# A bilinear layer's two factors as one product of halves: seven multiplications in place of eight

## The chip, the cores and the metric

The kernel runs on one core of a Trainium2 chip. The metric is the device time of one execution, in microseconds (us). Three runs of the kernel before took 1200.35, 1203.59 and 1203.63 us; their median is 1203.59 us. A profile was taken of one more execution. In it every engine is seen separately: PE is the matrix engine (PEld its weight loads), DVE the vector engine, ACT the scalar engine, POOL the GpSimd engine, SP the engine that issues most transfers. A fixed program stands in each engine's queue and is worked off in order; engines wait for each other by semaphores.

## The reference, cut to what matters

Three layers follow each other on 4352 rows of 512 numbers (34 tiles of 128 rows):

```python
x = attention(x, state)                       # 8 x 8 heads, 512 + 32 positions each
x = moe(x)                                    # every row goes to one of 8 experts:
                                              #   relu(row @ w1[e]) @ w2[e], times a gate
a, b = x @ w1, x @ w2                         # both 512 -> 1024: the two factors
out = ((a * b) @ w3) @ w_out                  # 1024 -> 1024 -> 512
```

The kernel multiplies w3 and w_out into one matrix "wo" (1024 x 512) while the attention runs, so that the last layer is `(a * b) @ wo`. The rows' gates are squared and put on at the very end, and rows lie in the experts' order until the output is scattered back.

All matrix products are in 32 bits. Each operand is held as a pair, high part and rest (`split`, lines 169 to 172: ACT casts the high part, DVE subtracts to get the rest), and a product takes three matmuls: high by high, high by rest, rest by high (`passes`, lines 174 to 180).

## The kernel before, in words

Three stages run one after the other.

- The attention and the routing, to about 200 us. The change doesn't touch them.
- The experts, from about 200 to 625 us. Ten units of rows go through them: eight "quads" of 4 tiles (512 rows, or 576 in four of them, where 64 rows of another tile ride along) and two single tiles. `quad_first` makes 8 hidden chunks (one PSUM bank of the four called A each, or two with 288 columns each), ACT and DVE take them out; `quad_second` makes 4 output chunks in the two banks called C, which ACT copies out and writes to `y_T` in DRAM. After each chunk `fill` (line 1096) puts a piece of other work into the program. These pieces (`convert_wab`, `write_wab`, lines 913 to 924) fetch the bilinear weights, which come as 64-bit words, 512 columns at a time, turn them into 32 bits and write them to `wab_rows` in DRAM.
- The bilinear layer, from 630 us to the end. Between the two stages stands a branch (line 1192, `tc.If`), which is taken only if the rows need more than 38 tiles in all.

The bilinear stage holds all weights in on-chip memory, as pairs. It takes the rows in a first block of 2 tiles (256 columns) and eight of 4 tiles (512 columns). For each block and each of the 8 groups of 128 factor columns (f) it makes two products, pB (factor a) and pC (factor b), each of 4 chunks of 128 x 3 matmuls, ACT copies pB, DVE multiplies by pC, the product is split, and one step later 4 x 3 matmuls add `(a * b) @ wo` to four banks "po". At the block's end the four po are scaled by the gates and scattered to the output rows by indirect transfers from POOL (lines 1340 to 1349). Beside this, in its first blocks, DVE works out where each row goes (`places`, lines 1311 to 1323): 34 small matmuls "pput" and a run of DVE instructions.

What stands in which order in an engine's queue is set by a scheduler that plays the program with estimated times, under the constraints in the code (`issue_after`, data and buffers). SP, ACT and POOL issue transfers, each in its own order. A buffer with `bufs=1` is written again only when all readers of its last content are done, transfers included.

Of the kernel before, what the change touches and what calls it, by code (L numbers as in the profile page):

```python
# [52 lines left out]
def tile_attention_moe_bilinear(  # L53
# [54 lines left out]
    )  # L108
    TQ = PLUS
# [44 lines left out]
    wab_rows = dram.tile([2, DM, FF], F32, name="wab_rows")  # L154
# [19 lines left out]
    def passes(o, l, r, start, stop, here=False):  # L174

        for i, (a, b) in enumerate(((0, 0), (0, 1), (1, 0))):
            m = nc.tensor.matmul(o, l[a], r[b], start=start and i == 0, stop=stop and i == 2)  # L177
            if here:
                tc.keep_in_program_order(m)
        return m  # L180
# [6 lines left out]
    def load_f32(pool, name, src, tag, bufs, temps=None, tmp=2):  # L187

        n = src.shape[1]
        w = pool.tile([P, n], F32, tag=tag, name=name, bufs=bufs)  # L190
        if src.dtype != I64:
            nc.sync.dma_start(out=w, in_=src)
            return w
        raw = wr_raw.tile([P, n], I64, tag="raw", name=name + "_raw", bufs=RAW)
        eng("q_raw", 0, "sync").dma_start(out=raw, in_=src)
# [95 lines left out]
    c3 = ctx.enter_context(ExitStack())  # L291
    with ExitStack() as c1:
# [386 lines left out]
        c2.close()  # L679
        rings.append(Lines(c3.enter_context(tc.tile_pool(name="wr0", bufs=RING0, reuse_waits="tile"))))  # L680
        xp = Lines(c3.enter_context(tc.tile_pool(name="xp", bufs=3, reuse_waits="tile")))
# [191 lines left out]
    with ExitStack() as c2:  # L873
# [22 lines left out]
        def gate():  # L896
# [4 lines left out]
            gt = e3.tile([P, 2, NTT], F32, name="gt", bufs=1)  # L901
# [3 lines left out]
            zr = e3.tile([P, NTT], F32, name="zr", bufs=1)  # L905
# [7 lines left out]
        def convert_wab(i):  # L913

            i, j = divmod(i, 2)
            w, k = divmod(i, KD)
            at = slice(k * P, (k + 1) * P), slice(j * 512, (j + 1) * 512)
            t = load_f32(e3, f"wab{i}_{j}", (wa, wb)[w][at], "wab", 1, None, 1)
            unwritten.append((wab_rows[w][at], t))

        def write_wab():
            for o, t in unwritten:
                nc.scalar.dma_start(out=o, in_=t)
            unwritten.clear()

# [4 lines left out]
        def rows(tiles, n, gidx=gidx, s0=0):  # L930
# [4 lines left out]
                xp.tile([P, KD, QN if quad else P], F32R, tag=f"x{quad}{j}", name=f"x{j}_{s}", bufs=1 if quad else 2)  # L935
# [151 lines left out]
        converted = iter(range(4 * KD))  # L1087
        fills = itertools.cycle(kn("fills", "cw--"))

        def next_of(items, n, todo):  # L1090
            for i in itertools.islice(items, n):
                todo(i)

# [6 lines left out]
        def fill_():  # L1100
            if next(calls) < kn("from", 8):
                return
            c = next(fills)
            if c == "c":
                next_of(converted, 1, convert_wab)
            if c == "w":
                write_wab()

        def rows_T(pool, first, n, bufs):

            hl = [
                pool.tile([P, KD, QN if pool is xp else 512], F32R, tag=f"xTrue{j}", name=f"y{j}_{first}", bufs=bufs)
                for j in range(2)
            ]
            for k in range(KD):
                y = xp.tile([P, n], F32, tag="xg", name=f"yt{first}_{k}", bufs=4)
                nc.sync.dma_start(out=y, in_=y_T[:, k, first : first + n])
                split(*both(hl, slice(None), k, slice(0, n)), y)
            return hl
# [40 lines left out]
        for c, n in steps:  # L1160
            if c == "f":
                first_of(n)
            else:
                if n + 1 == len(units):
# [3 lines left out]
                    ahead = rows_T(xp, 0, P * (QT // 2), 1)  # L1168
# [3 lines left out]
        next_of(converted, 4 * KD, lambda i: (convert_wab(i), write_wab()))  # L1172
        c4.close()

        wab = [
            [
                chunk(f"wab{i}_{k}", wab_rows[i, k * P : (k + 1) * P].rearrange("p (h f) -> p h f", h=2))
                for k in range(KD)
            ]
            for i in range(2)  # L1180
        ]
        wo = [
            chunk(f"wo{k}", wo_rows[2 * k * P : 2 * (k + 1) * P].rearrange("(h p) f -> p h f", p=P))
            for k in range(KF // 2)
        ]


        if not kn("used", 1):
            used = nc.values_load(total, min_val=0, max_val=MAXT)
        e2 = Lines(c2.enter_context(tc.tile_pool(name="e2_more", bufs=2, reuse_waits="tile")))  # L1190
        e4 = Lines(c2.enter_context(tc.tile_pool(name="e4", bufs=2, reuse_waits="tile")))
        with tc.If(used > T0):  # L1192
# [6 lines left out]
            def run(tiles):  # L1199
                for s in tiles:  # L1200
                    u = QUADS + s - TB
                    e = expert(u)
                    w = load1(u, e, e4, 2), load2(u, e, e4, 2)
# [9 lines left out]


    with ExitStack() as c2:
        b2 = Lines(c2.enter_context(tc.tile_pool(name="b2", bufs=2, reuse_waits="tile")))
        blocks = [range(max(t, 0), t + NC_) for t in range(QT // 2 - NC_, NTT, NC_)]
        acc = {}
        ridx = b2.tile([P, NTT], I32, name="ridx", bufs=1)
        gd = b2.tile([P, NTT], F32, name="gd", bufs=1)  # L1220

        PIECE, LOOK = 6, 9

        spare = oh.rearrange("p t e -> p (t e)")
        place = spare[:, 0:NTT]
        block, within = [
# [82 lines left out]
        def places():  # L1311
# [7 lines left out]
            for a in pieces:  # L1319
                put(a, o)  # L1320
                if a % (2 * PIECE):
                    yield
            yield taken(o)

        def nothing():
            while True:
                yield
# [84 lines left out]
```

## Time and profile before

| what | value |
| --- | --- |
| median of three runs | 1203.59 us (1200.35 to 1203.63) |
| the profiled execution | 1204.63 us, span in the trace 1202.8 us |
| mean granted TensorE clock | 0.989 of 2.4 GHz |
| PE busy | 1154.7 us, 96% |
| DVE, ACT, POOL busy | 515.6, 426.3, 183.4 us (43, 35, 15%) |
| expert stage ends, bilinear stage starts | 625.03 us, 630.27 us |
| last matmul ends | 1192.20 us |
| DRAM read and written | 97.03 MB, 33.55 MB |

How to read it: PE is busy nearly all the time, so a row's worth lies in what it makes PE do or wait for. A matmul's duration in the trace overlaps with its neighbours', so the price of one is taken from the distance between the starts of groups, not from its own length. An ACT or DVE row with a number in square brackets had its engine idle that long, and the arrow names what ended the wait.

### The profile page before, as it was taken

Reading aid. Unit: us, or ns where it says so; the run is one execution under the profiler, and the core shown is the slowest. Engines: PE = TensorE matmul, PEld = TensorE weight load, DVE = VectorE, ACT = ScalarE, POOL = GpSimd, SP = SyncE. Lnnn points to the kernel's source line nnn. Section 1 sums busy time; section 2 is a strip of 40 time slices with the busy share of each in tenths; the row PEclk is TensorE's granted clock in tenths of the full one; section 3 lists DMA queues with packets and bytes.
Section 4 is the critical chain, followed back from the end, with each engine's and each line's share of the span. In section 5 each row is a group of like instructions: output and inputs, shape, how many; then the busy total and the mean of one; then the engine's idle time right before and its main releaser. Section 6 shows DMA issues by size and latency. Waiting matters only on the chain.

```text
span 1202.8 us, 17604 instructions
## 1 busy us (share of the span) xinstructions
PE 1154.7 (96%) x6928; PEld 984.1 (82%) x6928; DVE 515.6 (43%) x999; ACT 426.3 (35%) x764; POOL 183.4 (15%) x183
## 2 busy tenths in 40 slices
PE   6898999999999999999989999999999999999996
PEld 4665777989999999888869888888888888888885
DVE  4999796543545454544347513112221312121211
ACT  3787544433545444544332212121121212121111
POOL 2655235102121112010000001010000101010101
PEclk9899999999999999999999999999999999999998
DMA  7776427545475546574332101001020202000000
GB/s 220 232 242 216 136 89 253 175 146 166 142 235 192 185 141 227 190 236 136 110 124 72 53 1 65 7 35 35 1 71 1 70 1 71 1 35 1 36 1 35
DMA packets 64700, 131.82 MB, mean 110 GB/s; under 512 B 11488, under 2 KB 22240, under 8 KB 64608
## 3 DMA queue, kind: packets, MB, share of 16 engines
q1 hardware_dynamic: 48864, 98.32, 25.3%
q0 software_dynamic: 5632, 18.35, 4.4%
q10 hardware_dynamic: 10112, 13.93, 3.2%
q8 instruction: 56, 0.92, 0.3%
q14 instruction: 36, 0.29, 0.1%
HBM read 97.03 MB, written 33.55 MB: 109 GB/s over the span
## 4 chain that ended last, share of the span: by engine, by line
issue 54%; PE 24%; DVE 8%; DMA 7%; ACT 3%; POOL 2%; SPq 0%; POOLq 0%; ACTq 0%; another core or an unknown queue 0%; DVEq 0%
PE py L177 10%; PE ph L177 9%; PE pwo L177 2%; DMA wab_raw<-in_moe_w 2%; POOL out L1348 2%; DMA raw<-in_moe_w 2%; DVE w L172 1%; DMA wu_raw<-in_moe_w_out 1%; ACT w L171 1%; PE pxr L636 1%; PE pxg L947 1%; DMA wab_rows<-wab 1%; DMA x<-in_x 1%; DVE ohlo L256 1%; DMA w_raw<-in_moe_w 1%
## 5 line engine op out<-in xcount | busy, mean ns | idle before, releaser
L1369 DVE TENSOR_TENSOR sa<-sa,pC 128x512 f32<-128x512 f32 (+1 forms) x72 | 47.3, 657 | 377.8 <-PE pC L177 332.4
L177 PE MATMUL pB<-y,w_wab 128*128 128x512 f32 (+1 forms) x864 | 200.1, 380 | 5.2 <-DVEq L1192 5.2
L177 PE MATMUL pC<-y,w_wab 128*128 128x512 f32 (+1 forms) x864 | 198.2, 378 | 0.4 <-ACTq L1192 0.4
L177 PE MATMUL po<-w_wo,ab 128*128 128x512 f32 x816 | 197.7, 390 | 0.0
L177 PE MATMUL ph<-x,w 128*128 128x288 f32 (+2 forms) x1248 | 195.2, 316 | 1.8 <-DVE h L969 1.7
L177 PE MATMUL py<-h,w 128*128 128x288 f32 (+1 forms) x1152 | 195.2, 328 | 1.0 <-ACT y L1031 1.0
L177 PEld LDWEIGHTS ph<-x,w 128*128 128x128 f32 x1248 | 179.7, 188 | 14.3 <-DVE h L969 2.9
L177 PEld LDWEIGHTS py<-h,w 128*128 128x128 f32 x1152 | 174.0, 188 | 16.4 <-ACT y L1031 1.6
L177 PEld LDWEIGHTS pB<-y,w_wab 128*128 128x128 f32 x864 | 157.9, 190 | 36.0 <-ACT y L1019 5.6
L177 PEld LDWEIGHTS pC<-y,w_wab 128*128 128x128 f32 x864 | 157.0, 189 | 30.7 <-ACTq L1192 0.7
L177 PEld LDWEIGHTS po<-w_wo,ab 128*128 128x128 f32 x816 | 152.4, 188 | 31.0
L172 DVE TENSOR_TENSOR w<-raw,w 128x1024 fp32r<-128x1024 f32 x80 | 95.8, 1223 | 111.4 <-ACT w L171 110.8
L1368 ACT COPY sa<-pB 128x512 f32<-128x512 f32 (+1 forms) x72 | 40.6, 563 | 259.9 <-PE pB L177 253.9
L1348 POOL DMA_INDIRECT out<-o,ridx x34 | 35.1, 1032 | 615.2 <-DVE o L1347 475.8
L171 ACT CAST ab<-sa 128x512 fp32r<-128x512 f32 (+1 forms) x72 | 42.9, 596 | 181.5 <-DVE sa L1369 181.5
L171 ACT CAST w<-raw 128x1024 fp32r<-128x1024 f32 x80 | 81.8, 1050 | 50.8 <-DMA raw<-in_moe_w 43.7
L969 DVE SCALAR_TENSOR_TENSOR h<-ph,h 128x288 fp32r<-128x288 f32 (+2 forms) x104 | 50.8, 502 | 61.8 <-ACT h L968 61.4
L968 ACT ACTIVATE h<-ph 128x288 fp32r<-128x288 f32 (+2 forms) x104 | 44.0, 446 | 62.1 <-PE ph L177 45.8
L172 DVE TENSOR_TENSOR ab<-sa,ab 128x512 fp32r<-128x512 f32 (+1 forms) x72 | 47.6, 661 | 34.8 <-ACT ab L171 34.8
L941 POOL DMA_INDIRECT xg<-x_rows,gidx x38 | 45.4, 1194 | 101.6 <-PE pxg L947 96.0
L177 PE MATMUL pwo<-wu,w3T 128*128 128x512 f32 x192 | 50.6, 413 | 1.6 <-POOL w3T L172 1.1
L221 POOL TENSOR_TENSOR wab<-wab,wab_top 128x512 int32<-128x512 int32 x16 | 20.6, 1290 | 187.8 <-DVE wab_top L214 161.1
(262 smaller groups left out, 997.1 us busy)
## 6 DMA issues: line engine op xcount, KB each, us to landing
raw<-in_moe_w SPq DMA_DIRECT2D x80, 512.0 KB, 4.4
x<-in_x SPq DMA_DIRECT2D x32, 256.0 KB, 5.6
w_raw<-in_moe_w SPq DMA_DIRECT2D x16, 512.0 KB, 4.1
x_rows<-xr SPq DMA_DIRECT2D x32, 256.0 KB, 2.7
wab_raw<-in_moe_w SPq DMA_DIRECT2D x16, 512.0 KB, 5.9
yt<-y_T SPq DMA_DIRECT2D x32, 256.0 KB, 3.9
y_T<-y ACTq DMA_DIRECT2D x16, 288.0 KB, 3.8
wu_raw<-in_moe_w_out SPq DMA_DIRECT2D x8, 512.0 KB, 6.1
```

The costliest lines, as they stand in the source:

```text
L171: nc.scalar.copy(hi, src)
L172: (engine or nc.vector).tensor_tensor(lo, src, hi.bitcast(F32), op=ALU.subtract)
L177: m = nc.tensor.matmul(o, l[a], r[b], start=start and i == 0, stop=stop and i == 2)
L221: nc.gpsimd.tensor_tensor(wi, wi, top, op=ALU.add)
L256: nc.vector.tensor_scalar(oh_lo, lane, lo[:, t : t + 1], None, op0=ALU.is_equal)
L636: nc.tensor.matmul(t, aT[g][:, c, :], st_d[:, b % (B // 2), g], start=True, stop=True)
L941: gathered = nc.gpsimd.indirect_dma_start(out=x[0:r], out_offset=None, in_=x_rows, in_offset=bass.IndirectOffsetOnAxis(ap=gidx[0:r, t - s0 ...
L968: nc.scalar.activation(hl[0], src, AF.Relu)
L969: nc.vector.scalar_tensor_tensor(out=hl[1], in0=src, scalar=0.0, in1=hl[0].bitcast(F32), op0=ALU.max, op1=ALU.subtract)
L1348: m = nc.gpsimd.indirect_dma_start(out=out, out_offset=bass.IndirectOffsetOnAxis(ap=ridx[:, t : t + 1], axis=0), in_=o, in_offset=None,)
L1368: behind = [nc.scalar.copy(sa, pab[0])]
L1369: behind += [nc.vector.tensor_tensor(sa, sa, pab[1], op=ALU.mult)]
```

## The change

Factor a and factor b are seen as one product of a 2 x 2 matrix of blocks with another: A11, A12 are the two halves of w1 (by input columns 0 to 255 and 256 to 511), A21, A22 those of w2; B11, B21 are the halves of the rows' columns for the first half of a block's rows, B12, B22 for its second half. The four results are a and b for the first and the second half of the rows. Winograd's form of Strassen's scheme gets them from seven products of halves, where the direct way takes eight, with four sums of weights (S1 to S4), four of rows (t1 to t4), and seven additions behind.

- Rows are taken in blocks of 7, 7, 7, 7 and 6 tiles, so a product has 448 columns (384 in the last block) and 2 chunks x 3 matmuls.
- The sums of the weights are made once, in the expert stage (`operands`), split into pairs there, and all seven operands are written to `w_rows` in DRAM: per f one piece of 128 x 3584 numbers. The bilinear stage fetches this piece anew for every f of every block, into two buffers.
- The sums of the rows are made per block (`sums_of`), by DVE for the first block and by POOL for the others, and all seven are split.
- The products' additions are on DVE and POOL (`products`).
- Of a block's 7 tiles, four po go along as before; the other three are made at the block's end from stored a * b.
- `places` moves from the bilinear stage into the fill pieces of the last experts.
- The branch for more tiles moves behind the bilinear stage, and makes it once more if it is taken.

```diff
@@ expert stage
-        def convert_wab(i):
-            i, j = divmod(i, 2)
-            w, k = divmod(i, KD)
-            at = slice(k * P, (k + 1) * P), slice(j * 512, (j + 1) * 512)
-            t = load_f32(e3, f"wab{i}_{j}", (wa, wb)[w][at], "wab", 1, None, 1)
-            unwritten.append((wab_rows[w][at], t))
+        def halves(blocks, at, name):
+            hl = [e3.tile([P, 4, P], F32R, tag=f"wh{j}", name=f"wh{j}_{name}", bufs=1) for j in range(2)]
+            n = blocks.shape[1]
+            split(*both(hl, slice(None), slice(0, n)), blocks)
+            f, kk, first = at
+            for j in range(2):
+                unwritten.append((w_rows[f, :, j, kk, first : first + n], hl[j][:, 0:n].bitcast(F32)))
+        def operands():
+            for f in range(KF):
+                for kk in range(2):
...
+                    w = load_f32(
+                        e3, "wab" + name, [wa_, wb_[:, 1], wb_[:, 0]], "wab", 1, None, 1
+                    ).rearrange("p (m n) -> p m n", n=P)
+                    a11, a12, a22, a21 = [w[:, i] for i in range(4)]
+                    yield
...
+                    add = nc.gpsimd.tensor_tensor
+                    add(s1, a21, a22, op=ALU.add)
+                    add(s3, a11, a21, op=ALU.subtract)
+                    add(s2, s1, a11, op=ALU.subtract)
+                    add(s4, a12, s2, op=ALU.subtract)
+                    halves(w[:, 0:3], (f, kk, 0), "w" + name)
+                    yield
+                    write_wab()
+                    yield
+                    halves(sums, (f, kk, 3), "s" + name)
+                    yield
+                    write_wab()
-        fills = itertools.cycle(kn("fills", "cw--"))
+        fills = itertools.chain(operands(), places())
@@ bilinear stage
+            def load_w(s, f):
+                t = wp.tile([P, 2, 2, NP, P], F32R, tag="w", name=f"w{s}_{f}", bufs=2)
+                nc.sync.dma_start(out=t.bitcast(F32), in_=w_rows[f])
+                w_t[s, f] = t
...
+                t1 = less(1, b12, b11)
+                t2 = less(2, b22, t1)
+                put(0, b11)
+                put(1, t1)
+                t3 = less(3, b22, b12)
+                put(2, t2)
+                t4 = less(4, t2, b21)
+                put(3, t3)
+                put(4, b21)
+                put(5, b22)
+                put(6, t4)
...
+                p1 = product(0, "B", A11, "1")
+                s1 = temp(xp, "s1", "xFalse0")
+                nc.scalar.copy(s1, p1)
+                p5 = product(1, "B", S1, "5")
+                s5 = temp(xp, "s5", "xFalse1")
+                nc.scalar.copy(s5, p5)
+                p6 = product(2, "C", S2, "6")
+                vector(u2, s1, p6, op=ALU.add)
+                p7 = product(3, "C", S3, "7")
+                vector(u3, u2, p7, op=ALU.add)
+                gpsimd(b2, u3, s5, op=ALU.add)
+                p3 = product(5, "B", S4, "3")
+                vector(u4, u2, p3, op=ALU.add)
+                gpsimd(a2, u4, s5, op=ALU.add)
+                gpsimd(ab[:, n : 2 * n], a2, b2, op=ALU.mult)
+                p2 = product(4, "B", A12, "2")
+                vector(a1, s1, p2, op=ALU.add)
+                p4 = product(6, "C", A22, "4")
+                vector(b1, u3, p4, op=ALU.subtract)
+                vector(ab[:, 0:n], a1, b1, op=ALU.mult)
...
+            for s, n in enumerate(BLOCKS):
+                first, more = sum(BLOCKS[:s]), s + 1 < len(BLOCKS)
+                ab, po = [], {}
+                for f in range(KF):
+                    ab.append(products(s, f, x))
...
+                    for i in range(QT if f else 0):
+                        if f == 1:
+                            po[i] = bank("A", f"po{first + i}")
+                        out_of(po[i], ab[f - 1][0], i, f - 1)
+                    if f + 2 < KF or more:
+                        load_w(*((s, f + 2) if f + 2 < KF else (s + 1, f + 2 - KF)))
+                    if f == 1 and more:
+                        y = load_y(s + 1)
+                if more:
+                    x = sums_of(y, s + 1)
+                for i in range(QT, min(n, QT + 2)):
+                    po[i] = bank("C", f"po{first + i}")
...
-        with tc.If(used > T0):
...
+    bilinear(y0, "out")
+    with tc.If(used > T0):
...
+        bilinear(load_y(0), "again")
```

The change moves instructions on all engines. Three places matter below. In all of them the last number of a name is the buffer's.

In ACT's queue, in the expert stage, the pieces that ready the bilinear weights stand among the casts of hidden chunks (h0). Before, a converted piece (wab3_0) is written out by one transfer, and nothing of the same buffer follows closely:

```order
L206 ACTIVATE wab3_0_top_4899<-wab3_0_raw_4897 128x512
L968 ACTIVATE h0_2_1_4761<-ph2_1_288_4821 128x288
L220 ACTIVATE wab3_0_4896<-wab3_0_raw_4897 128x512
L968 ACTIVATE h0_2_2_4763<-ph2_2_0_4836 128x288
L968 ACTIVATE h0_2_2_4763<-ph2_2_288_4851 128x288
L923 DMA wab_rows_67<-wab3_0_4896 128x512
L968 ACTIVATE h0_2_3_4765<-ph2_3_0_4866 128x288
```

Now two splits follow each other in one buffer (wh0, for its rest wh1), each with two transfers:

```order
L177 CAST wh0_w7_1_6895<-wab7_1_6863 128x384
L1013 ACTIVATE h0_6_2_6798<-ph6_2_0_6846 128x512
L939 DMA w_rows_67<-wh0_w7_1_6895 128x384
L939 DMA w_rows_67<-wh1_w7_1_6896 128x384
L177 CAST wh0_s7_1_6931<-sums7_1_6890 128x512
L939 DMA w_rows_67<-wh0_s7_1_6931 128x512
L1013 ACTIVATE h0_6_3_6800<-ph6_3_0_6875 128x512
L939 DMA w_rows_67<-wh1_s7_1_6932 128x512
```

The cast of the second split (wh0_s7_1) now stands right behind the transfers that empty the same buffer, and the next hidden chunk (h0_6_3) behind that cast.

The second place is ACT's queue where the expert stage ends: y7_0 to y7_3 are the last four output chunks of the experts. Before, the branch follows them:

```order
L1019 COPY y7_0_7139<-py7_0_7039 128x512
L1020 REGISTER_ALU
L1020 DMA y_T_69<-y7_0_7139 128x512
L1019 COPY y7_1_7142<-py7_1_7040 128x512
L171 CAST w0_wo3_7221<-raw_wo3_7219 128x1024
L1020 ISA
L1020 DMA y_T_69<-y7_1_7142 128x512
L1019 COPY y7_2_7145<-py7_2_7041 128x512
L1020 ISA
L1020 DMA y_T_69<-y7_2_7145 128x512
L1019 COPY y7_3_7148<-py7_3_7042 128x512
```

Now the bilinear stage's first casts (x0 to x6 are the seven sums of the first block's rows) and the copies out of its first products (s1, s5) stand among and behind them; y7_0 is just ahead of this piece:

```order
L1064 COPY y7_1_7539<-py7_1_7437 128x512
L1065 ISA
L1065 DMA y_T_69<-y7_1_7539 128x512
L177 CAST x0_0_0_7585<-y0_0_7423 128x896
L177 CAST x1_0_0_7589<-t1_0_7581 128x896
L1064 COPY y7_2_7542<-py7_2_7438 128x512
L1064 COPY y7_3_7545<-py7_3_7439 128x512
L1065 ISA
L1065 DMA y_T_69<-y7_2_7542 128x512
L1065 ISA
L1065 DMA y_T_69<-y7_3_7545 128x512
L1403 COPY s1_0_0_7639<-p1_0_0_7632 128x448
```

What moved: no branch stands here any more, and the casts x0 and x1 come behind the copies of two of the last expert chunks. After s1 follow s5 and the casts x2 to x6, so behind all four.

The third place is DVE's queue where the first block of 7 tiles ends and the second begins (nothing of before answers to it: there a block's first matmuls need no sums). po6 is the seventh tile's bank, p2, p6, p3 the second block's first products:

```order
L1441 TENSOR_SCALAR o4_8506<-po4_8435,L_75 128x512
L1418 TENSOR_TENSOR a1_1_0_8545<-s1_1_0_8557,p2_1_0_8596 128x448
L1441 TENSOR_SCALAR o6_8540<-po6_8515,L_75 128x512
L1409 TENSOR_TENSOR u2_1_0_8575<-s1_1_0_8557,p6_1_0_8568 128x448
L1414 TENSOR_TENSOR u4_1_0_8544<-u2_1_0_8575,p3_1_0_8586 128x448
L1411 TENSOR_TENSOR u3_1_0_8543<-u2_1_0_8575,p7_1_0_8577 128x448
```

The instruction that frees p3's bank (u4) stands behind the one that takes p6 out (u2). On PE the second f's p1, which goes into p3's bank, stands directly behind p6.

## Rows read from the trace of the kernel before

**Rows 1.** The page: busy time, share, instructions of PE and PEld and others.
```profile
PE 1154.7 (96%) x6928; PEld 984.1 (82%) x6928; DVE 515.6 (43%) x999; ACT 426.3 (35%) x764; POOL 183.4 (15%) x183
```

**Rows 2.** Stretches: length, busy of PE, PEld, DVE, ACT, POOL; clock; DMA share; GB/s.
```profile
603.11:625.03 21.92, 21.92 (x97) 17.84 (x95) 9.38 (x12) 8.20 (x13) 0.00 (x0) 1.00 0.38 131
630.27:633.54 3.27, 2.90 (x12) 2.60 (x12) 0.00 (x0) 0.00 (x0) 0.00 (x0) 0.50 0.23 85
640.00:667.00 27.00, 27.00 (x191) 24.64 (x190) 24.80 (x60) 6.76 (x16) 0.00 (x0) 1.00 0.13 40
667.00:1192.00 525.00, 525.00 (x2331) 434.38 (x2330) 120.24 (x182) 102.48 (x172) 31.96 (x31) 1.00 0.08 28
1192.20:1202.80 10.60, 0.01 (x1) 0.00 (x0) 0.12 (x1) 0.69 (x1) 2.91 (x3) 0.60 0.26 99
```

**Rows 3.** PE in order of time where the bilinear stage begins: start, length, what.
```profile
603.11 21.92 PE L177 MATMUL py<-h,w 128*128 128x512 f32 x96
630.27 2.90 PE L177 MATMUL pB<-y,w_wab 128*128 128x256 f32 x12 [5.24 <-DVEq L1192]
...
635.54 1.60 PE L177 MATMUL pB<-y,w_wab 128*128 128x256 f32 x12
636.98 1.60 PE L177 MATMUL pC<-y,w_wab 128*128 128x256 f32 x12
```

**Rows 4.** PE in order of time, two groups of a full block.
```profile
1178.44 2.88 PE L177 MATMUL po<-w_wo,ab 128*128 128x512 f32 x12
...
1181.16 2.88 PE L177 MATMUL pB<-y,w_wab 128*128 128x512 f32 x12
```

**Rows 5.** ACT in order of time where the expert stage ends.
```profile
624.99 0.34 ACTq L1020 DMA_DIRECT2D y_T<-y  x1
...
629.37 0.58 ACT L1019 COPY y<-py 128x512 f32<-128x512 f32 x1 [3.00 <-SPq L1192]
```

**Rows 6.** Groups by line, 640 to 1192 us: count, busy, mean ns; idle before.
```profile
L172 DVE TENSOR_TENSOR ab<-sa,ab 128x512 fp32r<-128x512 f32 x64 | 44.2, 691 | 34.4 <-ACT ab L171 34.3
...
L171 ACT CAST ab<-sa 128x512 fp32r<-128x512 f32 x64 | 39.7, 620 | 169.1 <-DVE sa L1369 169.1
```

**Rows 7.** Groups by line, whole span.
```profile
L575 POOL TENSOR_TENSOR an<-a,s 128x512 f32<-128x512 f32 x16 | 17.9, 1138 | 25.6 <-DVE s L572 13.2 <-ACT xr L137 9.9 <-DVE L L644 1.8
...
L220 ACT ACTIVATE wab<-wab_raw 128x512 int32<-128x512 uint32 x16 | 10.6, 663 | 12.8 <-DMA wab_rows<-wab 12.8
```

**Rows 8.** Transfers: a queue's bytes and share; issues, KB each, us to landing.
```profile
q1 hardware_dynamic: 48864, 98.32, 25.3%
...
raw<-in_moe_w SPq DMA_DIRECT2D x80, 512.0 KB, 4.4
...
out<-o,ridx POOLq DMA_INDIRECT x34, 2.7
...
yt<-y_T SPq DMA_DIRECT2D x4, 128.0 KB, 2.0
```

**Rows 9.** The tile wab_rows: its transfers' landing.
```profile
DMA to landing us min/median/max: 2.8/4.5/5.8
```

**Rows 10.** What line 1192, the branch, issued: count, ns, first and last start.
```profile
L1192 POOLq INC_SWDGE_SEM  x1: 944/944/944, 545.8 to 545.8; - x1
...
L1192 DVEq COMPARE_BRANCH  x1: 72/72/72, 626.6 to 626.6; - x1
L1192 DVEq EVENT_SEMAPHORE  x1: 21/21/21, 630.1 to 630.1; - x1
```

**Rows 11.** The last 17 us in order of time.
```profile
1186.60 5.60 PE L177 MATMUL po<-w_wo,ab 128*128 128x512 f32 x24
...
1191.23 0.97 POOL L1348 DMA_INDIRECT out<-o,ridx  x1 [54.74 <-DVE o L1347]
...
1195.06 0.97 POOL L1348 DMA_INDIRECT out<-o,ridx  x1 [0.30 <-issue]
```

**Rows 12.** Whom PE waited for from 205 to 626 us: total, times, longest.
```profile
PE ph L177 <- DVE h L969: 1.7, 3, 1.3
```

More of the change, by code (lines that the diff above doesn't have):

```diff
@@ L108, in tile_attention_moe_bilinear @@
     )
+    BLOCKS = [7, 7, 7, 7, 6]
+    assert sum(BLOCKS) == NTT
     TQ = PLUS
@@ L1100, in fill_ @@
         def fill_():
[L1101 to L1119, printed above, removed]
+            if next(calls) >= kn("from", 7):
+                next(fills, None)
@@ new lines, in tile_attention_moe_bilinear, with more_tiles @@
+        PIECE, LOOK = 6, 9
+        spare = oh.rearrange("p t e -> p (t e)")
+        place = spare[:, 0:NTT]
+        block, within = [
+            spare[:, i : i + NTT // 2].bitcast(F16) for i in (NTT, NTT + NTT // 2)
+        ]
+        values = spare[:, 2 * NTT : 2 * NTT + 5 * NTT // 2].bitcast(BF16).rearrange(
+            "p (j t) -> p j t", j=5
+        )
+        def more_tiles():
+            n = MAXT - T0
+            at = xp.tile([P, NTT, n], F16, tag="xFalse0", name="more_at", bufs=1)
+            nc.vector.tensor_tensor(at, bt(tile_h[:, T0:]), be(hi, n), op=ALU.is_equal)
+            some = small([P, n], F32, "more_some")
+            nc.vector.tensor_reduce(some, at.rearrange("p t n -> p n t"), axis=AX.X, op=ALU.add)
+            some_h = small([P, n], F16, "more_h")
+            nc.vector.tensor_copy(some_h, some)
+            pv = bank("B", "pmore")
+            nc.tensor.matmul(pv[:, 0:n], ones, some_h, start=True, stop=True)
+            count = small([P, n], F32, "more_count")
+            nc.vector.tensor_copy(count, pv[:, 0:n])
+            end = small([P, n], F32, "more_end")
+            nc.vector.tensor_tensor_scan(end, ones[:, 0:n], count, filled, op0=ALU.mult, op1=ALU.add)
+            nc.vector.tensor_tensor(first_row[:, T0:], end, count, op=ALU.subtract)
@@ new lines, in taken, with places @@
+        def taken(o):
+            got = xp.tile([P, 5, NTT], F32, tag="xFalse1", name="got", bufs=1)
+            nc.vector.tensor_copy(got, o.rearrange("p (j n) -> p j n", j=5))
+            nc.vector.scalar_tensor_tensor(
+                out=ridx, in0=got[:, 0], scalar=float(P), in1=got[:, 1], op0=ALU.mult, op1=ALU.add
+            )
+            nc.vector.tensor_tensor(gd, got[:, 2], got[:, 3], op=ALU.add)
+            nc.vector.tensor_tensor(gd, gd, got[:, 4], op=ALU.add)
+        def places():
+            yield more_tiles()
+            for a in range(0, NTT, 2 * LOOK):
+                yield [look_up(i) for i in range(a, min(NTT, a + 2 * LOOK), LOOK)]
+            yield parts_of()
+            o = bank("B", "pput")[:, 0 : 5 * NTT]
+            pieces = list(range(0, NTT, PIECE))
+            for a in pieces:
+                put(a, o)
+                if a % (2 * PIECE):
+                    yield
+            yield taken(o)
@@ new lines, in tile_attention_moe_bilinear, with load_y @@
+        ridx = L.rearrange("p t e -> p (t e)")[:, 0:NTT].bitcast(I32)
+        gd = L.rearrange("p t e -> p (t e)")[:, NTT : 2 * NTT]
+        fills = itertools.chain(operands(), places())
+        def load_y(s):
+            first, n = sum(BLOCKS[:s]) * P, BLOCKS[s] * P // 2
+            y = []
+            for j in range(2):
+                t = xp.tile([P, KD * QN], F32, tag=f"xTrue{j}", name=f"y{s}_{j}", bufs=1)
+                y.append(t[:, 0 : KD * n].rearrange("p (k n) -> p k n", k=KD))
+                nc.sync.dma_start(out=y[j], in_=y_T[:, :, first + j * n : first + (j + 1) * n])
+            return y
```

354 lines of the change are left out of this document (172 added, 182 removed).

## The prediction, written before the changed kernel was run

> **What bounds the kernel now.** I read the page first: PE is busy 96% of the span [rows 1], so the time is PE's work plus its few gaps. The table by stretches says where: from 667 to 1192 us PE is without a gap at full clock while DVE and ACT are busy a fifth of the time [rows 2]. That stage is bound by matmul columns alone, and the change takes columns away there. Then PE in order of time at the seam between the stages: experts end at 603.11 + 21.92 = 625.03, the first pB starts at 630.27 after 5.24 us of idling behind the branch [rows 3]. In the 3.27 us after that the granted clock was 0.50, the lower of the two levels (1.2 GHz), after an idle PE [rows 2].
>
> Prices of a matmul: two groups of 12 with 512 columns start 2.72 us apart, 226.7 ns each [rows 4]; two with 256 columns start 1.44 us apart, 120.0 ns [rows 3]. The line through both is 13.3 ns plus 0.4167 ns a column, so 200.0 ns for 448 columns, 173.3 for 384, 133.3 for 288.
>
> The stage before, checked by that: 64 pairs (8 blocks, 8 f) of 24 matmuls are 1536 x 226.7 = 348.2; the short block 192 x 120.0 = 23.0; 816 for po 185.0; the 35 small ones of places 2.4. Sum 558.6. From 630.27 to the last matmul's end at 1192.20 [rows 11] are 561.9; the 3.3 left are mostly the slow clock (the first two groups took 630.27 to 635.54, 2.4 more than 2 x 1.44). With the gap, 567.2 from the experts' end.
>
> **The change part by part.**
>
> *Columns.* Per f and block 7 products x 2 chunks x 3 = 42 matmuls. Four blocks of 448: 1344 x 200.0 = 268.8. One of 384: 336 x 173.3 = 58.2. The po stay, 185.0. Sum 512.0.
>
> *Beside it, per f.* PE needs 42 x 0.200 + 12 x 0.2267 = 11.1 us. DVE gets six operations of 448 and splits of 512 and 384: at 691 ns per 512 [rows 6] 6 x 0.60 + 0.69 + 0.52 = 4.8. ACT gets two copies and two casts, 2.2 at 620 ns per 512 [rows 6]. POOL gets three operations, 3 x 1.0 at 1138 ns per 512 [rows 7]. All lie under PE; each bank is taken out two products (2.4 us) before it is wanted.
>
> *The weights.* Each f fetches 1.835 MB (1792 KB) into one of two buffers, from the end of f's products to the start of f+2's: 11.1 us to land. No row shows such a transfer. One end: queue 1 moved 98.32 MB in 25.3% of the span, 323 GB/s while it works [rows 8]: 5.7 us. Other end: 128 KB landed in 2.0 us, 512 KB in 4.4 [rows 8]; 160 KB a us gives 2.0 + 10.4 = 12.4. I take the queue's rate plus the small transfer's 2.0: 7.7, since the single chunks waited among other traffic. That is hidden, 0; gain is none either. The end 12.4 is a rival below.
>
> *The start.* The gap of 5.24 goes with the branch; late next is ACT's queue. ACT casts x0 only after the copy and transfer of y7_1, which ended 0.3 us after the experts' end [rows 5], and 896 columns cost 1.1 on ACT and 1.2 on DVE [rows 6]. So p1 really runs from 2.4, p5 until 4.7. Then comes y7_3: its buffer waits for y7_1's transfer, and in the trace that copy started 4.3 us after the end, at 629.37 [rows 5]. Behind it stand two transfers, s1, s5 and the casts x2 to x6, each with a DVE rest: p6 and p7 run from 8 to 10, p2, p3, p4 end near 13.8 instead of 8.4. The splits of wo, whose fetches stand behind the next block's rows on SP, hold ACT again in f = 1, by some 3 us. I take 8.5 lost; bounds 0 (PE waits for nothing) and 16 (the same at half clock).
>
> *Block seams.* At a seam u4 frees p3's bank only after u2, which waits for p6, and p1 of the next f follows p6 directly on PE: 2 x 0.60 of DVE, 1.3 with the hand-over. Four seams: 5.2; bounds 0 and 10. POOL's sums for the next rows (896 columns, 2.0 each) lie under the 84 matmuls (19 us) at a block's end.
>
> With 1.0 for small things as before, the stage is 512.0 + 8.5 + 5.2 + 1.0 = 526.7 against 567.2: **-40.5**.
>
> *The expert stage.* Places bring their 2.4 us of PE along. Its DVE work, some 19 us (24.8 busy in 27 us where it ran [rows 2], against 0.23 per us later), falls into the last two quads, where DVE was busy 9.4 of 21.9 [rows 2]: it fits. The pieces for the weights grow: ACT gets 48 more transfers of 0.34 [rows 5] and 32 casts, 33 us in some 300. The heavier point is a wait: wh0 and wh1 have one buffer, so the second cast of each of 16 pieces waits for a write to land, 4.5 us in the median [rows 9], and the next hidden chunk stands behind it. Before, a like wait on the buffer wab cost ACT 12.8 us in all [rows 7] and PE waited for DVE 1.7 us in the whole stage [rows 12]. The four A banks cover 4.5 us; the two C banks of a 576-row quad cover one of 24 x 0.133 = 3.2, leaving 1.3. All 16 exposed would be 21, none 0. Eleven pieces fall into such quads, a third of the fills beside C banks: 4 x 1.3 = 5. **+2.4 + 5.**
>
> Here the Trainium skill would add: SBUF — State Buffer, "Who interferes with whom", says a DVE instruction with two SBUF inputs and a GpSimd instruction that reads SBUF block each other for a whole instruction. The rows before show no such pair by itself. By that rule the 64 new additions on POOL (128 columns, an estimate of 0.28 us each from rows 7) could hold DVE's splits up by 18 us; that would make the second rival likelier. I count nothing for it.
>
> *The end.* Six tiles leave POOL 1.28 us apart (1191.23 to 1195.06 in three steps [rows 11]) where four did, from 2.4 us before PE's end on, so POOL ends 5.0 after PE rather than 3.8; with the four output buffers' wait, +1.5. Then the branch: on DVE it took from 626.6 to 630.1, and POOL issued 0.94 us for it [rows 10], partly beside the last output's landing (2.7 [rows 8]). I take 2, between 0 and 4. **+3.5.**
>
> Sum: -40.5 + 7.4 + 3.5 = -29.6. The profiled execution took 1204.6, so 1175.0; the median of the runs lies 1.0 below it: **1174**.
>
> **Rivals.**
>
> 1. *The cover holds everywhere*: start, seams and casts cost PE nothing. For it: PE's waits in the expert stage were tiny [rows 12] although ACT waited there. Against it: ACT's order at the stage seam, which no speed of a transfer changes. With the seams (5.2) and the casts' 5 gone and half the start left (4 of 8.5): 1174 - 5 - 5 - 4 = 1160; with the whole start gone too 1155.
> 2. *The expert stage pays*: ACT, held by 16 write landings and 48 more issues, becomes late for PE. For it: one buffer where two splits follow each other, and chunks behind them in the same queue. Against: ACT was at 37% in the stretch at 603 us [rows 2]. All 16 exposed, 21 for 5: 1190.
> 3. *The weights' transfer becomes the bound*, the case that ends slower. Place: load_w in every f from the third on, 6 a block, 30 in all. At the 12.4 us of the upper end PE waits 1.3 in 24 of them and 2.4 in the six of the last block (10.0 us per f): 46 us, 1174 + 46 = 1220. It decides from the point where the 30 waits eat up 29.6: L = 12.0 us. For it: no transfer of this size in the trace, and chunks of 512 KB took 4.4. Against: queue 1's own rate. The Trainium skill, DMA: Bandwidth & Descriptors, "Anatomy of one DMA", gives 2.0 us plus bytes at 436 GB/s for a transfer from POOL's queue, an estimate of 6.2 us here, by which this rival falls away; my chance doesn't rest on it.
>
> **How the numbers follow.** The forecast with small shifts (1166 to 1183) gets 0.55, rival 1 0.17, rival 2 0.18, rival 3 0.07; 0.03 for a landing between, around 11.9 us, that just eats the gain. Three runs before spread by 0.3%, so 0.3% (3.6 us) is what can be told from no change. Faster 0.90, same 0.03, slower 0.07. The range goes from 1157 (leaving out the lower part of rival 1, 0.08) to 1190 (leaving out rival 3, the 0.03 and a little of rival 2, 0.12).
>
> **What would show it.** In the profile after: groups of six matmuls with 448 columns starting 1.20 us apart, 1680 matmuls for the products in place of 1728; PE's idle time before p1, p6 and p7 of the first block 5 to 9 us in sum, released by ACT casts x; 1.3 us before p1 at each seam, released by DVE u4; w's landing 6 to 9 us with no PE wait for it; in the expert stage PE waits of a few us for ACT y; the last matmul's end some 14 us before the span's. Wrong is the sum if a product's six matmuls take clearly more than 1.20 us, the mechanism if PE waits for w or w_rows in every f.

## The result, and the profile after

The changed kernel takes **1185.68 us** (median of 4 runs, 1182.64 to 1187.32) where the kernel before took 1203.22 in the same session: ratio 0.9856, interval 0.9831 to 0.9882. That is 17.5 us faster, inside the range, 11.7 slower than the forecast. Its profiled execution took 1187.3 us with a span of 1185.4.

The page, with the lines that answer [rows 1] and [rows 8]:

```profile
PE 1123.0 (95%) x6880; PEld 986.2 (83%) x6880; DVE 660.9 (56%) x1206; ACT 448.7 (38%) x807; POOL 396.3 (33%) x383
...
L183 PE MATMUL p<-x,w 128*128 128x448 f32 (+1 forms) x1680 | 350.2, 363 | 8.7 <-DMA w<-w_rows 7.1
...
w<-w_rows SPq DMA_DIRECT2D x40, 1792.0 KB, 7.1
```

There are 1680 matmuls for the products in place of 1728, and the weights land in 7.1 us in the median (7.7 was taken; rival 3 needed 12.0, by its own terms 11.9). In 40 fetches PE waited for one only, the first.

The stretches, answering [rows 2] (busy us and count of PE, PEld, DVE, ACT, POOL; then the granted clock, DMA share, GB/s):

```profile
633.93:641.03 7.10, 0.00 (x0) 0.03 (x1) 3.19 (x3) 2.75 (x4) 0.00 (x0) 0.69 0.97 369
641.03:645.85 4.82, 4.82 (x12) 3.77 (x12) 0.00 (x0) 0.53 (x1) 0.00 (x0) 0.50 0.98 388
645.85:665.00 19.15, 16.72 (x66) 14.40 (x66) 13.97 (x20) 9.62 (x15) 3.82 (x3) 0.79 0.78 284
665.00:1168.70 503.70, 503.70 (x2421) 449.36 (x2419) 241.28 (x358) 118.12 (x201) 208.11 (x163) 1.00 0.44 162
1168.70:1185.40 16.70, 0.00 (x1) 0.00 (x0) 0.75 (x1) 0.69 (x1) 3.88 (x4) 0.62 0.22 82
```

PE stands from 633.93 to 641.03, then runs at the lower level (0.50) or a mix until 665, and then has no gap up to its last matmul. The end is 16.7 us long, where it was 10.6 (1192.20 to 1202.8).

PE in order of time at the start of the last stage, answering [rows 3]:

```profile
621.19 12.74 PE L183 MATMUL py<-h,w 128*128 128x512 f32 x55
641.03 4.82 PE L183 MATMUL p<-x,w 128*128 128x448 f32 x12 [7.11 <-DMA w<-w_rows]
647.31 14.40 PE L183 MATMUL p<-x,w 128*128 128x448 f32 x54 [1.46 <-ACT x L177]
662.58 2.33 PE L183 MATMUL po<-wo,aa 128*128 128x512 f32 x9 [0.88 <-ACT aa L177]
664.75 1.38 PE L183 MATMUL p<-x,w 128*128 128x448 f32 x6
```

SP's waits say what held that fetch (line 1332 is load_w):

```profile
SPq L1332 <- PE py L183: 21.3, 1, 21.3
```

The fetch was ready to go at 612 us, but its buffer lies in the space of the experts' last second-layer weights, which py reads until 633.93. So it was issued at 633.79 and landed 7.1 us later.

Against the forecast's own terms, by the profiled execution (forecast 1175.0, measured 1187.3):

| term | forecast | measured | from |
|---|---|---|---|
| experts' end, against 625.03 | +7.4 | +8.9 | 633.93 |
| start, over its columns | 8.5 | 15.6 | 633.93 to 664.75, less 66 x 0.2 and 9 x 0.2267 |
| seams | 5.2 | 0 | no PE wait from 665 on |
| small things, dearer matmuls | 1.0 | 7.2 | 664.75 to 1168.70 is 503.95, columns 496.75 |
| end | +3.5 | +6.1 | 16.7 for 10.6 |

The differences are +1.5, +7.1, -5.2, +6.2 and +2.6, together 12.2 of the 12.3 that are missing. In the first term two things stand against each other: here the experts also began 1.1 us earlier than before, so the stage itself grew by 10.0 us (424.3 to 434.3). Its first matmuls, before and after:

```profile
200.75 0.72 PE L177 MATMUL ph<-x,w 128*128 128x256 f32 x4
```

```profile
199.63 0.72 PE L183 MATMUL ph<-x,w 128*128 128x256 f32 x4
```

### The profile page after: what moved, and what is told of

Same layout as the page of the kernel before. It is cut to its first block, busy times and chain, and to the rows that moved or that the text cites. A ratio compares the mean times of both kernels' runs of the same rounds, so it can differ in the third digit from the quotient of the medians.

```text
span 1185.4 us, 18194 instructions
## 1 busy us (share of the span) xinstructions
PE 1123.0 (95%) x6880; PEld 986.2 (83%) x6880; DVE 660.9 (56%) x1206; ACT 448.7 (38%) x807; POOL 396.3 (33%) x383
## 5 line engine op out<-in xcount | busy, mean ns | idle before, releaser
L183 PE MATMUL p<-x,w 128*128 128x448 f32 (+1 forms) x1680 | 350.2, 363 | 8.7 <-DMA w<-w_rows 7.1
L183 PEld LDWEIGHTS p<-x,w 128*128 128x128 f32 x1680 | 315.2, 190 | 35.9 <-issue 7.5
L183 PEld LDWEIGHTS ph<-x,w 128*128 128x128 f32 x1248 | 179.4, 188 | 12.5 <-DVE h L1014 1.2
L1412 POOL TENSOR_TENSOR b<-u,s 128x448 f32<-128x448 f32 (+1 forms) x40 | 47.7, 1191 | 279.5 <-DVE u L1411 279.5
L183 PE MATMUL po<-wo,aa 128*128 128x512 f32 x480 | 123.1, 393 | 0.9 <-ACT aa L177 0.9
L183 PEld LDWEIGHTS po<-wo,aa 128*128 128x128 f32 x480 | 89.7, 188 | 18.0 <-ACT aa L177 1.5
L183 PE MATMUL po<-wo,ab 128*128 128x512 f32 x336 | 79.6, 390 | 0.0
L183 PEld LDWEIGHTS po<-wo,ab 128*128 128x128 f32 x336 | 62.9, 188 | 13.3 <-DVE o L1441 0.2
L1415 POOL TENSOR_TENSOR a<-u,s 128x448 f32<-128x448 f32 (+1 forms) x40 | 48.4, 1209 | 58.8 <-DVE u L1414 58.7
L1414 DVE TENSOR_TENSOR u<-u,p 128x448 f32<-128x448 f32 (+1 forms) x40 | 24.3, 607 | 64.1 <-PE p L183 63.9
L1416 POOL TENSOR_TENSOR ab<-a,b 128x448 f32<-128x448 f32 (+1 forms) x40 | 50.1, 1252 | 3.1
## 6 DMA issues: line engine op xcount, KB each, us to landing
raw<-in_moe_w SPq DMA_DIRECT2D x80, 512.0 KB, 4.3
w_raw<-in_moe_w SPq DMA_DIRECT2D x16, 512.0 KB, 4.1
```

The source lines that it names most:

```text
L1412: gpsimd(b2, u3, s5, op=ALU.add)
L1414: vector(u4, u2, p3, op=ALU.add)
L1415: gpsimd(a2, u4, s5, op=ALU.add)
L1416: gpsimd(ab[:, n : 2 * n], a2, b2, op=ALU.mult)
```

## The experiments

Theory: the first weight fetch, late by its place in memory, is the late start. Rivals: ACT's order alone is; the weights' traffic slows the matmuls; the branch's new place costs what the old one did.

**w_early** and **x_early** change the order of the last stage's pools, which are laid out one behind the other; x_early also moves block 0's casts.

```diff
-            wp, ap, xp0, op0, xp1, op1, aap, abp, tp = [
+            xp0, ap, op1, op0, wp, xp1, aap, abp, tp = [      # w_early
+            op1, ap, xp0, op0, wp, xp1, aap, abp, tp = [      # x_early
...
-                    split(*x[i], src)
+                    if s == 0:                                # x_early
+                        nc.vector.tensor_copy(x[i][0], src)
+                        nc.vector.tensor_tensor(x[i][1], src, x[i][0].bitcast(F32), op=ALU.subtract)
+                    else:
+                        split(*x[i], src)
```

> The pools of the last stage stand in another order, so that the two weight buffers lie where the last experts' first-layer weights lay (free from 613 us on) and not under their second-layer weights. Theory A (the first weight fetch, held until the experts' last matmul, sets the start): w lands before 622, PE's wait for it (7.1 us) goes; next late is the rest of x0 on DVE (ended 636.0), so the first product runs near 636, and then the casts x2 to x6 behind the copies s1 and s5 on ACT. The start then costs some 10 us over its columns instead of 15.6: about 1180. Rival B (ACT's order of casts sets the start, and the fetch only ended inside that time): first p6 moves by less than 1 us: 1185.

Measured: 1180.94 (1180.03 to 1181.98), ratio 0.9815 [0.9784, 0.9845]. PE in order of time in w_early:

```profile
625.84 9.23 PE L183 MATMUL py<-h,w 128*128 128x512 f32 x40
636.10 0.47 PE L183 MATMUL p<-x,w 128*128 128x448 f32 x1 [1.04 <-ACT x L177]
637.23 2.49 PE L183 MATMUL p<-x,w 128*128 128x448 f32 x11 [0.66 <-DVE x L178]
641.18 0.47 PE L183 MATMUL p<-x,w 128*128 128x448 f32 x1 [1.46 <-ACT x L177]
...
655.86 2.31 PE L183 MATMUL po<-wo,aa 128*128 128x512 f32 x9 [2.06 <-ACT aa L177]
658.00 1.38 PE L183 MATMUL p<-x,w 128*128 128x448 f32 x6
```

Theory A holds: the wait for w is gone, the first product is at 636.10 (636 was said), and what is late next is what the prediction had named, ACT's order of casts. From 635.07 to 658.00 the start now costs 22.93 - 15.24 = 7.7 us over its columns (some 10 was said). This is the start that the prediction priced at 8.5.

> As the one with the earlier weight buffers, but x0 and x1 lie in early free space too, and the first block's casts to the high halves are on DVE, which is idle from 623 to 634 us, instead of ACT behind the experts' last copies. Theory A': weights and ACT's order together were the whole start; PE goes from py to p without a wait, the granted clock stays 1.00, and the start costs 0 to 2 us over its columns instead of 15.6: about 1171. Rival B': other things are late next (the splits of wo on ACT, s1 and s5, DVE's own 20 us of splits): half is lost again, about 1178.

Measured: 1176.67 (1174.44 to 1180.12), ratio 0.9781 [0.9744, 0.9817]. PE goes straight from py to p, and then stops once:

```profile
634.85 3.00 PE L183 MATMUL p<-x,w 128*128 128x448 f32 x14
639.92 15.22 PE L183 MATMUL p<-x,w 128*128 128x448 f32 x64 [2.07 <-ACT s L1407]
```

The same stretch of ACT: two of the experts' copies wait for a buffer, and the product's copy s1 (line 1407) stands behind them.

```profile
635.71 0.59 ACT L1064 COPY y<-py 128x512 f32<-128x512 f32 x1 [1.06 <-DMA y_T<-y]
...
638.29 0.58 ACT L1064 COPY y<-py 128x512 f32<-128x512 f32 x1 [1.99 <-DMA y_T<-y]
...
639.34 0.53 ACT L1407 COPY s<-p 128x448 f32<-128x448 f32 x1 [0.47 <-ACT y L1064]
```

Neither sum came. From the experts' end (635.01) to 654.98 are 19.97 us, 4.4 over the 78 matmuls' columns, where theory A' allowed 0 to 2; rival B' was right that something else is late next, and its 1178 is the nearer one. This is the wait for one of two buffers that the prediction had expected for y7_3.

**x_early_y4** gives those copies four buffers.

```diff
-                    y = e2.tile([P, QN], F32, tag="y", name=f"y{u}_{f}", bufs=BY)
+                    y = xp.tile([P, DM], F32, tag="xg", name=f"y{u}_{f}", bufs=BX)
```

> x_early, with the experts' last four y copies in four buffers (those of the gathered rows, idle by then) instead of two. In x_early the copy s1 stood on ACT behind y_2 and y_3, which waited 1.06 and 1.99 us for a transfer, and PE waited 2.07 us for s1, after which the clock was low for some 4 us. Theory: that wait goes, the clock stays 1.00, the start costs under 1 us over its columns instead of 4.4: 1173. Rival: s1 is still late since ACT issues four transfers (0.34 each) ahead of it: half stays, 1175.

Measured: 1173.26 (1170.69 to 1178.06), ratio 0.9764 [0.9733, 0.9795]: as the theory had it. py ends at 633.95, and f = 0 runs without a wait:

```profile
633.78 13.97 PE L183 MATMUL p<-x,w 128*128 128x448 f32 x66
647.89 2.11 PE L183 MATMUL po<-wo,aa 128*128 128x512 f32 x8
```

13.94 us for columns of 13.2. The whole late start, 15.6 us, was thus two things one behind the other: a buffer under live weights, and ACT's queue. Of the 14.9 us that went, the medians show 12.4; one new wait came behind them, 1.02 us for the third weight fetch (under *Rival 3* below).

**no_refetch** tests whether the fetches slow the matmuls.

```diff
             def load_w(s, f):
+                if (s, f) > (0, 1):
+                    w_t[s, f] = first_w[f % 2]
+                    return
...
-                w_t[s, f] = t
+                w_t[s, f] = first_w[f] = t
```

> Leaves out the fetch of the weights after the first two: all products of the last stage use the first two weight tiles (the output is then not the reference's). Theory C (matmuls are slowed by what the fetches, 1792 KB every 11.4 us, do beside them): the spacing of a 448-column matmul falls from 202.8 to 200.0 ns and of a po from 228.4 to 226.7: 5 to 6 us less, 1180. Rival D (the extra 3 ns belong to the matmul and its groups): spacing stays at 202 to 203, the time within 1 us of 1185.7.

Measured: 1189.36 (1187.66 to 1195.91), ratio 0.9898 [0.9865, 0.9931]. Its stretches and PE's order:

```profile
700.00:800.00 100.00, 99.18 (x468) 87.47 (x467) 49.09 (x72) 24.19 (x40) 45.28 (x34) 1.00 0.10 37
```

```profile
691.09 5.11 PE L183 MATMUL p<-x,w 128*128 128x448 f32 x24
696.03 2.48 PE L183 MATMUL po<-wo,aa 128*128 128x512 f32 x10
...
702.46 5.11 PE L183 MATMUL p<-x,w 128*128 128x448 f32 x24
```

The DMA share falls from 0.44 to 0.10 and a pair of f and block still takes 11.37 us (691.09 to 702.46; 11.37 too in the changed kernel, 696.71 to 708.08). Theory C falls; rival D has the spacing right, but not the time, which it put within 1 us of 1185.7. Between the two profiled executions (1187.3 and 1189.4) the time rose by 2.0 us, and 1.7 of that are two waits of PE for output copies at seams; the medians, of two sessions, differ by 3.7, and the rest is open.

**products_twice** asks whether the dearer matmul is a matter of its column count or of the change of bank after every six matmuls.

```diff
-                    for k in range(2):
-                        passes(o, (w[:, 0, k, c], w[:, 1, k, c]), both(x[i], slice(None), k), k == 0, k == 1)
+                    for k in range(4):
+                        passes(o, (w[:, 0, k % 2, c], w[:, 1, k % 2, c]), both(x[i], slice(None), k % 2), k == 0, k == 3)
```

> The changed kernel with every product added up twice (12 matmuls into a bank in place of 6; the output is then not the reference's). Theory D1 (a matmul of 448 columns itself takes 202.7 ns where the line through 256 and 512 columns gave 200.0): the spacing stays at 202.5 to 203; a pair of block and f takes 84 x 202.7 + 2.73 = 19.8 us. Theory D2 (the extra 2.7 ns are a change of bank every six matmuls, 16 ns each): with 12 to a bank the spacing falls to 201.3, 19.6 us. The sum is about 1185.7 + 338 = 1524 either way; it is read from the spacing.

Measured once: 1514.82. PE in order of time:

```profile
859.73 17.19 PE L183 MATMUL p<-x,w 128*128 128x448 f32 x84
876.75 2.91 PE L183 MATMUL po<-wo,aa 128*128 128x512 f32 x12
879.50 17.19 PE L183 MATMUL p<-x,w 128*128 128x448 f32 x84
```

84 matmuls in 17.02 us are 202.6 ns each, as theory D1 has it. The straight line through 256 and 512 columns [rows 3, 4] is not the price at 448. The total came 9 us lower than expected, about what that sum took too much for the last block: 336 matmuls at 202.7 instead of 173.8 ns.

**no_branch**, **before_no_branch** and **branch_between** price the branch's two places. The first leaves out all behind the last stage, the second the branch between the stages in the kernel before, the third moves the block:

```diff
+    with tc.If(used > T0):
+        ...
     def bilinear(y, group):
...
     bilinear(y0, "out")
-    with tc.If(used > T0):
-        ...
-        bilinear(load_y(0), "again")
```

> Leaves out the branch for more tiles behind the last stage (it is not taken with these inputs). Theory E (the branch behind the outputs costs 4 us: its loads of the count, its hand-overs and POOL's 1.6 us of INC_SWDGE_SEM): from the last matmul to the end 12.5 us instead of 16.7: 1181.5. Rival F (the tail is six outputs 1.28 us apart on POOL with four buffers; the branch lies beside their landing): 16 us, 1185.

Measured: 1184.64 (1181.85 to 1187.19), ratio 0.9838 [0.9805, 0.987]. The tail is as theory E says, 11.9 us (12.5 was said), 4.8 less; the median is only 1.0 lower. In this profile the experts ended 4.4 us later (638.35): their stage began 2.1 later, at 201.72, and PE waited 8.3 us in it instead of 6.8. Why this kernel does both is not shown. So 4.8 is shown for the tail, not for the total. What the branch put there in the changed kernel, the last line being the end's drain:

```profile
1172.58 0.69 ACT L1439 ACTIVATE o<-po,L 128x512 f32<-128x512 f32 x1 [4.51 <-DMA out<-o,L]
1173.54 0.97 POOL L1442 DMA_INDIRECT out<-o,L  x1 [1.05 <-DVEq L1489]
```

```profile
L1489 POOLq INC_SWDGE_SEM  x1: 1628/1628/1628, 1177.0 to 1177.0; - x1
```

```profile
L1540 POOLq DRAIN  x3: 40/107/5959, 1178.6 to 1185.1; - x3
```

The sixth output waited 4.51 us for one of four buffers (2.44 without the branch), and POOL's hand-over of the branch (1.63) begins at 1177.0, 3.5 us after that output was issued (the six land in 2.8 to 4.8, median 3.2), so the drain starts only at 1178.6.

> The kernel before, with its branch between the stages left out (it is not taken with these inputs): what the branch costs beside eight products. Theory G (the branch was the gap): the 5.24 us before the first pB shrink to under 1 and the slow clock behind them goes: about 7 us less, 1196. Rival (other things are late at the same place, the fetched chunks of the weights and ACT's copies): the gap stays over 3 us, 1201.

Measured: 1194.52 (1193.39 to 1199.76), ratio 0.9934 [0.9918, 0.9951]. Theory G holds: the 5.24 of [rows 3] and the slow clock behind it go, and the median falls by 7.5 us (7 was said).

```profile
605.82 21.92 PE L177 MATMUL py<-h,w 128*128 128x512 f32 x96
627.58 1.60 PE L177 MATMUL pB<-y,w_wab 128*128 128x256 f32 x12
```

> The changed kernel with the branch put back between the two stages (without the second pass of the last stage in it), so that the seven products stand alone. Theory H (the place of the branch is worth nothing or less: the late fetch of the weights covers it between the stages, and behind the outputs it stands open): the tail falls from 16.7 to 12 us, the wait before the first product stays at 7 to 8 us: about 1181. Rival I (the fetch can be issued only behind the branch, some 5 us later): the tail falls as well, but the first product waits 12 us: about 1186. The move of the branch is worth 5 us or more only if this one is over 1190.

Measured: 1190.6 (1188.94 to 1191.92), ratio 0.9909 [0.9892, 0.9925]. Rival I's mechanism is there, with a different sum:

```profile
650.37 15.33 PE L183 MATMUL p<-x,w 128*128 128x448 f32 x66 [13.68 <-DMA w<-w_rows]
```

The fetch went out behind the branch, and the wait doubled; but the casts were done by then, so the start cost 15.6 us over its columns, the same as with the branch moved. The tail fell to 11.9. Three waits for output copies at seams (2.6) and a later experts' end (636.69; PE waited 9.2 us in that stage instead of 6.8) took that back, and why they came is not shown. So seven products with the branch where it was gain 11.4 us. By the medians of two sessions the move adds some 5; the profiled executions (1188.9 and 1187.3) differ by 1.6.

**pieces_apart** changes the experts' stage alone.

```diff
-            hl = [e3.tile([P, 4, P], F32R, tag=f"wh{j}", name=f"wh{j}_{name}", bufs=1) for j in range(2)]
...
+            hl = [
+                xp.tile([P, KD, P], F32R, tag=f"xFalse{j}", name=f"wh{j}_{name}", bufs=1) if at[2] else
+                e3.tile([P, 4, P], F32R, tag=f"wh{j}", name=f"wh{j}_{name}", bufs=1)
+                for j in range(2)
+            ]
```

> The changed kernel, with the halves of the sums s1 to s4 in two other buffers (those of the single tiles' rows) instead of the ones that the halves of A11, A12, A22 are still being written from. Theory J (ACT's 15 waits for such a write, 26.3 us, are what PE waits 6.0 us for in the experts' stage): ACT's wait for them falls under 5 us, PE's wait for ACT y to 2 us, the experts end 4 us earlier: 1181.5. Rival K (the waits move to the single tiles' rows, or PE's waits come from ACT's work as a whole): PE's waits stay at 4 to 7 us, 1185.

Measured: 1176.84 (1175.34 to 1177.89), ratio 0.9786 [0.977, 0.9803]: theory J's mechanism, at twice its price. ACT waits for no such write any more. The waits in the changed kernel's experts' stage, first PE's, then ACT's:

```profile
PE py L183 <- ACT y L1076: 6.0, 7, 2.5
```

```profile
ACT wh_s L177 <- DMA w_rows<-wh_w: 26.3, 15, 3.8
```

and in pieces_apart:

```profile
PE py L183 <- ACT wab L232: 0.4, 1, 0.4
```

```profile
611.42 12.74 PE L183 MATMUL py<-h,w 128*128 128x512 f32 x55
631.79 4.82 PE L183 MATMUL p<-x,w 128*128 128x448 f32 x12 [7.63 <-DMA w<-w_rows]
```

The experts end at 624.16 instead of 633.93. Of the 9.8, 6.0 are PE's waits (6.8 in all less 0.8). For part of the rest, here are 25 us of the changed kernel, and what the longest of the waits does:

```profile
340.00:365.00 25.00, 22.00 (x155) 21.47 (x154) 9.73 (x14) 9.01 (x18) 6.44 (x8) 0.93 0.65 214
```

```profile
349.54 11.34 PE L183 MATMUL py<-h,w 128*128 128x288 f32 x72 [2.49 <-ACT y L1076]
360.71 0.56 PE L183 MATMUL ph<-x,w 128*128 128x288 f32 x3
```

72 matmuls of 288 columns took 11.17 us instead of 72 x 0.1333 = 9.6, and the granted clock was 0.66 from 350 to 355. A wait of 2.49 us so cost 1.6 more in granted clock. Behind the waits of 0.2 to 1.0 us in the same stage the granted clock was 1.00. The remaining 2.2 us are not accounted for.

**all_three** puts x_early_y4 and pieces_apart together.

> The changed kernel with the three cures together: weights and block 0's rows in space that is free early with block 0's casts on DVE, four buffers for the experts' last y copies, and the sums' halves in the single tiles' buffers. Theory L (the late start and the hold-up of ACT in the experts' stage are separate losses and add): from 1173.3 the 9 us of pieces_apart come off: 1164.5, ratio to the kernel before 0.968. Rival (they share a wait, or the earlier experts' end only finds the weights or rows later): 1170.

Measured: **1163.07** (1161.64 to 1163.99), ratio 0.9672 [0.9654, 0.969], faster than both kernels. Theory L holds (1164.5 was said): the losses add. PE's waits from the experts' stage to the end:

```profile
PE p L183 <- DVE ab L1429: 1.2, 1, 1.2
```

From the experts' end (621.55) to the last matmul (1143.15) are 521.6 us; less the columns' 512.0, 0.7 at the start and this 1.2, the dearer matmuls are still 7.7.

## Why the prediction was right, and where it lost 12 us

*What bounds the kernel, and the columns:* right. From 665 us on the stage is PE's columns without a gap. By the forecast's prices they fell by 44.2 us (558.6 less the 2.4 of places, to 512.0), and all of that came but for the 7.2 by which the matmuls were dearer.

*The start:* the step that failed. The prediction took the first product at 2.4 us, behind ACT's casts, and the weights as covered. It had seen that a weight buffer is refilled from the end of f's products on, but had not asked what lies in that memory before f = 0: the first fetch waits for py as the cast waits for the copies. PE stood 7.1 us instead of 2.4, and behind that came 24 us of low or mixed clock, so the start cost 15.6 for 8.5. Repaired by w_early alone, it costs 7.7: the mechanism, ACT's order, was right, but second in line. That 7.7 lies so near 8.5 is in part luck. The 8.5 took y7_3's copy as waiting for y7_1's transfer until 4.3 us after the experts' end, but in [rows 5] the row of that copy names the branch (SPq L1192) as what it waited for. Without the branch (before_no_branch) it starts 2.5 us after the end, at 630.27 with the experts' end at 627.74:

```profile
630.27 0.59 ACT L1019 COPY y<-py 128x512 f32<-128x512 f32 x1 [1.19 <-DMA y_T<-y]
```

In w_early that copy did not wait at all: of the 7.7 us, 5.8 are PE's waits for casts and splits, and the granted clock was 1.00 throughout. The slow clock of the changed kernel's start thus came with the long wait for w, and the forecast had it only in its upper bound.

*The matmul price:* mis-sized. 448 columns take 202.6 ns, not 200.0 (products_twice, no_refetch): 1278 x 2.6 ns = 3.3 of the 7.2 us. The last block's 384 columns took 173.8 (24 in 4.17 us) and fit the line. The rest sits where products and po alternate: a pair split in four groups takes 11.37 us, 42 x 0.2026 + 12 x 0.2267 are 11.23. In products_twice a pair in two groups takes 19.77 us, only 0.03 over 84 x 0.2026 + 12 x 0.2267. No run changed the grouping by itself.

*The seams:* wrong, 0 for 5.2, and it is luck that this hid a part of the late start. At a seam PE has the block's remaining po to do, and they stand between the products:

```profile
742.03 0.97 PE L183 MATMUL p<-x,w 128*128 128x448 f32 x4
742.84 5.41 PE L183 MATMUL po<-wo,ab 128*128 128x512 f32 x23
748.08 2.88 PE L183 MATMUL po<-wo,aa 128*128 128x512 f32 x12
```

Rival 1 held here, and only here.

*The experts' stage:* mechanism right (second splits waiting for writes), size nearly. The forecast had 4 waits of 1.3 exposed, 5 us; there were 7, of 0.2 to 2.5, 6.0 us in all. Missing was the clock's answer to the longest of them. Against before, the stage grew by 10.0, 7.6 of it beside the 2.4 of places, and this 7.6 is to be set against the forecast's 5. The 9.8 that pieces_apart takes off are more, for they hold waits such as the kernel before had too (PE waited 2.7 us there in all). Both lie well under rival 2's 21.

*The end:* 6.1 for 3.5. The branch costs 4.8 there (2 was taken), its hand-over not beside the last landing but behind it. The six outputs cost 1.3 (1.5 was taken).

*Rival 3* (the weights' transfer): the 40 fetches landed in 6.9 to 8.8 us, 7.1 in the median, with no wait after the first. The estimate worked out from the Trainium skill (DMA: Bandwidth & Descriptors, "Anatomy of one DMA"), for a transfer from POOL's queue, was 6.2; these, from SP's queue, took 0.9 more. The rival is nearer than this median says: in x_early_y4, where f = 0 has no wait left, the third fetch was issued at 644.52 beside fetches of wo and took some 11 us until PE could go on.

```profile
655.58 5.19 PE L183 MATMUL p<-x,w 128*128 128x448 f32 x24 [1.02 <-DMA w<-w_rows]
```

## What to carry to other kernels

When a stage begins with fetches into new buffers, ask whose memory that is and when its last reader is done: a transfer hidden in every later turn can be bare in the first, and the order of the pools alone moved it. A wait on a TensorE-bound path can cost more than itself: behind 2.49 us here (the changed kernel's row under pieces_apart) the lower granted clock took 1.6 us more, while behind the waits of 1 us and less in the same stage the clock stayed at 1.00. The length of a wait did not decide it alone: behind 2.07 us in x_early the granted clock was 0.66 (640 to 645), behind 2.06 us in w_early 1.00 (655 to 660). So read the granted clock behind each wait before giving it a price. Price a matmul from rows of its own width: the line through its neighbours was 1.3% low at 448 columns and 0.3% at 384.

## What was not expected of the hardware

A VectorE (DVE) subtraction beside a GpSimd (POOL) one, both on two SBUF inputs, took three times as long. In the changed kernel, first DVE's row, then POOL's:

```profile
669.63 2.08 DVE L178 TENSOR_TENSOR wo<-rwo,wo 128x512 fp32r<-128x512 f32 x1
```

```profile
668.65 2.51 POOL L1362 TENSOR_TENSOR t<-y,y 128x896 f32<-128x896 f32 x1 [0.63 <-DVE wo L178]
```

Alone a DVE operation of this form took 0.69 [rows 6]. From 650 us on this holds throughout: of the splits of 512 columns that stand singly in the trace, the 39 with no POOL addition, subtraction or multiplication beside them took 0.68 to 0.69 us, and the two with one 1.79 and 2.08; of 384 columns, 31 took 0.54 to 0.56 and the one beside POOL 2.48. The Trainium skill, SBUF — State Buffer, "Who interferes with whom", says that such a pair contends, and these rows agree. The 18 us that the rule gave for the experts' stage did not come. The splits of the sums run behind POOL's additions and took 676 to 694 ns; the 16 splits of the other halves (384 columns) run beside them and took 785 to 802 ns, some 0.24 us more each than alone, 4 us of DVE time in all. None of the delays after 665 us reached PE.
